# A gated convolution block's gradients: gradient of h interleaved with the weight gradients, and two queues held in program order

## The chip, the cores and the metric

The kernel runs on one core of a Trainium2 chip. The metric is the device time of one execution in microseconds. The core has five engines with a queue of instructions each: PE (TensorE, matmuls into PSUM), DVE (VectorE, elementwise), ACT (ScalarE, copies and functions), POOL (GpSimd, here mostly a queue that starts DMAs) and SP (SyncE, which only starts DMAs). PEld is PE's weight load, which runs beside the matmuls.

## The reference

All outputs of a forward pass and of its gradient (`jax.vjp`), S = 2048, D = 1024, F = 3584, bf16:

```python
x  = A_q
xn = layernorm(x)
# s: gated long convolution
kv = shift4(A_k, shift_k) * A_v
y  = irfft(rfft(kv, 2S) * rfft(ssm_k, 2S))[:S] + kv * ssm_D
s  = xn * y
# g: gated linear unit
h  = (xn @ w_gate) * (xn @ w_up)
g  = silu(h @ w_down)
out = x + s * g
# returned: out and the gradients of A_q, A_k, A_v, shift_k, ssm_k, ssm_D, w_gate, w_up, w_down
```

The Fourier transforms are done as matmuls with tables on PE (eight residues of the position), and short butterflies on VectorE.

## The kernel before

The program is one stream of traced instructions over all engines. A planner then puts each engine's instructions in an order, by priority and by its own estimates of when inputs are ready; on the chip each engine runs its queue in that order. `tc.high_priority` lifts instructions in it, `tc.issue_after(ins)` keeps a block's instructions behind `ins` on that engine.

The helpers `ld`, `st` and `sta` start a DMA from SP, GpSimd and ACT. `cld` is `st`. Nearly all VectorE work goes through `tt` (L199) and `stt` (L255), so these two lines carry many groups of the profile, which are told apart by their tiles.

Stages, in order:

1. Layer norm, and gate and up projections (L569, tile psg), with the forward convolution spread among them.
2. Multiplication by w_down and the gate's gradient (L961, function `gate`). It writes DY (gradient of the convolution's output) and DBM (gradient of h @ w_down) to DRAM.
3. The weight gradients of gate and up. F is cut into 14 slabs of 256. For each slab, `dh_half` computes the gradient of h for one half of the positions: two groups (g) of two PSUM tiles of 16 matmuls each (L1085), copied by ACT to dht (L1087), and VectorE multiplies the saved gate and up values by dht in place (tiles U<-U,dht); then the half is stored to DGd. `dw_slab` then makes the slab's weight gradients: 8 groups of 16 matmuls (L1100) that read these products, one ACT copy each (L1105), and stores of wb from ACT's queue.
4. The gradient of w_down: 14 slabs of 4 groups of 16 matmuls (L1201), copied by ACT to wbs (L1203, four buffers) and stored from SP's queue. The saved h of a slab is loaded two slabs ahead, from ACT's queue (`load_h`, U<-Hd). Beside it, SP issues the transposing DMAs that the last stage needs (L1160, L1167), from slab 1 on; each slab's are held behind the last store of wbs.
5. The gradient of xn (L1224) and the layer norm's gradient, with the gradient of k (`dk_units`) among it.

The backward convolution (`conv_backward`) is a generator that stages 3 and 4 draw forward. After each group of matmuls `btick` counts 1 (one PSUM tile of `dh_half`, 16 matmuls) or 2 (a dw or down group), and `make_pump` traces as much of the generator as keeps its share done. A generator's yields are its weights in estimated VectorE microseconds. First `dy_forward` transforms DY (8 units of `fwd8`) into DYFd. Then 16 units follow (8 of kind v, 8 of kind h). A unit's `main` loads A and B, multiplies them on VectorE (`product`, steps of 2.3, 2.5, 2.5, 2.5, 2.5) and does the inverse butterflies (`inv8`). A unit's `tail` does the last matmuls (psY: L404 for v, L901 for h), ACT copies and stores. `staggered` starts a unit's tail within the next unit's main, once more than 6.0 of its weights are done, and then alternates the two. At slab 11 of stage 4, `bdrain` traces what is left.

The order around the change was, in each slab `sl`: dh_half(2 sl + 1), dh_half(2 sl + 2) for the next slab, then dw_slab(sl). The multiply was lifted by `high_priority(60)`.

Of the kernel before, what the change touches and what calls it, by code (L numbers as in the profile page):

```python
# [19 lines left out]
def build_kernel(  # L20
# [11 lines left out]
    nc = tc.nc  # L32
# [27 lines left out]
    def ld(out, in_):  # L60
        return nc.sync.dma_start(out=out, in_=in_)

    def st(out, in_):
        return nc.gpsimd.dma_start(out=out, in_=in_)

# [127 lines left out]
    def pr(t, i, j):  # L193
        if j > i:
            return t[:, i:j + 1:j - i, :]
        return t[:, i:(j - 1 if j > 0 else None):j - i, :]

    def tt(o, a, b, op):
        V.tensor_tensor(o, a, b, op)  # L199

# [52 lines left out]
    def stt(o, a, f, b):  # L253

        V.scalar_tensor_tensor(o, a, f, b, op0=MUL, op1=ADD)  # L255

    def fwd8(x, X, wp, psp):

        W = wp.tile([P, 16, 256], F32, name="W16")
        C = wp.tile([P, 4, 256], F32, name="W4")  # L260
        for i in range(2):
            SP = wp.tile([P, 2, 2, 512], F32, name="SP", bufs=2)
            for j in range(2):
                r = 2 * i + j
                ps = psp.tile([P, 2, 2, 256], F32, name="psF")
                cmm(ps[:, 0], T4[0], x, (r,))
                cmm(ps[:, 1], T4[0], x, (r + 4,))
                nc.scalar.copy(out=SP[:, :, j], in_=ps[:].rearrange("p s k x -> p s (k x)"))
                yield 0.1
            s, q = [SP[:, j].rearrange("p a (k x) -> p (a k) x", k=2) for j in range(2)]  # L270
            tt(W[:, 4 * i:4 * i + 4, :], s, q, ADD)
            tt(W[:, 4 * i + 8:4 * i + 12, :], s, q, SUB)
            yield 2.5
        tt(C[:], W[:, 0:4, :], W[:, 4:8, :], ADD)
        tt(W[:, 0:4, :], W[:, 0:4, :], W[:, 4:8, :], SUB)
        yield 2.4
        dft4(C[:], W[:, 0:4, :], X, 0)
        yield 2.8

        d0, d2r = W[:, 8:10, :], W[:, 13:11:-1, :]  # L280
        tt(C[:, 0:2, :], d0, d2r, ADD)
        tt(d0, d0, d2r, SUB)
        re, im = W[:, 10:15:4, :], W[:, 11:16:4, :]
        tt(C[:, 2:4, :], re, im, ADD)
        tt(W[:, 12:14, :], im, re, SUB)
        yield 2.8
        q, pr_ = C[:, 2:4, :], W[:, 13:11:-1, :]
        tt(W[:, 10:12, :], q, pr_, ADD)
        tt(W[:, 14:16, :], q, pr_, SUB)
        stt(pr(X, 2, 15), W[:, 10:15:4, :], C8, C[:, 0:2, :])  # L290
        stt(pr(X, 10, 7), W[:, 10:15:4, :], -C8, C[:, 0:2, :])
        yield 2.9
        stt(pr(X, 6, 11), W[:, 11:16:4, :], C8, d0)
        stt(pr(X, 14, 3), W[:, 11:16:4, :], -C8, d0)
        yield 1.5
    FWD8_W = 0.4 + 2 * 2.5 + 2.4 + 2.8 + 2.8 + 2.9 + 1.5

# [502 lines left out]
    def dy_forward(cx, cs):  # L800
        def load(ds):
            x = cx.tile([P, NB, P], BF16, name="dyx")
            cld(x[:], DYd[ds])
            return x
        nx = load(0)
        for ds in range(8):
            x = nx
            if ds < 7:
                nx = load(ds + 1)
            X = cs.tile([P, 16, 256], BF16, name="DX")  # L810
            yield from fwd8(x, X, cs, ps_c3)
            st(DYFd[ds], X[:])

    def conv_backward():
# [54 lines left out]
        for n in range(16):  # L869
            yield from staggered(main(n), tl, 6.0)  # L870
            tl = tail(n)
# [6 lines left out]
    def dkv_tail(ds, G, tiles, ew):  # L878
        v, ksh = tiles
        y = ew.tile([P, NB, P], BF16, name="yl")  # L880
        for rp in range(4):
            ps = inv8_rows(G, ps_y4[0], rp)
            nc.scalar.copy(out=by_res(y[:], rp), in_=rowps(ps))
        yield 0.4
        tt(v[:], v[:], y[:], MUL)
        tt(ksh[:], ksh[:], y[:], MUL)
        for c in range(2):
            cs_ = slice(8 * c, 8 * c + 8)
            st(DKSHd[ds, 1024 * c:1024 * c + 1024, :].rearrange("(u r) d -> u r d", r=8), v[:, cs_, :])
            st(o_dv[:, c, :, ds * P:(ds + 1) * P], ksh[:, cs_, :])  # L890
        yield 2.5

    def dh_tail(ds, G, ew):
        ho = ew.tile([P, 2, P, 8], BF16, name="yl")
        for c in range(2):
            for rq in range(2):
                ps = ps_y4[0].tile([P, 4, P], F32, name="psY")
                for i in range(4):
                    r = 4 * rq + i
                    for k in range(2):  # L900
                        nc.tensor.matmul(ps[:, i, :], G[:, 2 * r + k, c * P:(c + 1) * P], TI[:, 0, r, k, :],  # L901
                                         start=(k == 0), stop=(k == 1))
                nc.scalar.activation(ho[:, c, :, 4 * rq:4 * rq + 4].rearrange("p u r -> p r u"), ps[:], ACT.Copy, scale=WSC)
        yield 0.4
        nc.scalar.copy(out=ddo[:, ds:ds + 1], in_=ho[:, 0, 0, 0:1])
        st(o_dssmk[ds * P:(ds + 1) * P, :], ho[:].rearrange("p c u r -> p (c u r)"))
        yield 0.1

# [42 lines left out]

    C_TOTAL = 8 * FWD8_W + 16 * (PROD_W + INV8_W) + 8 * 1.4 + 8 * 2.9 + 8 * 0.5
    bpump, bdrain = make_pump(conv_backward(), C_TOTAL)

# [114 lines left out]
    def btick(n):  # L1069
        bcnt[0] += n  # L1070
        bpump((bcnt[0] - 10) / (BT - 10))

    def dh_half(k, wdt):

        sl, hf = divmod(k, 2)
        dgu = DGU[k]
        for g in range(2):
            bs = slice(4 * g, 4 * g + 4)
            dht = bg.tile([P, 4, SLW], BF16, name="dht", bufs=3)
            for e in range(2):  # L1080
# [6 lines left out]
                nc.scalar.copy(out=dht[:, 2 * e:2 * e + 2].rearrange("p b f -> p (b f)"), in_=ps[:])  # L1087
                flush(2)
                btick(1)
            with tc.high_priority(60):  # L1090
                tt(dgu[:, :, bs], dgu[:, :, bs], dht[:].unsqueeze(1).to_broadcast([P, 2, 4, SLW]), MUL)

        ld(DGd[sl, :, 1024 * hf:1024 * hf + 1024, :].rearrange("a (u b) f -> u a b f", u=P), dgu)
        return dgu

    def dw_slab(sl, dgus):
        for dc in range(DC):
# [8 lines left out]
            if dc % 2 == 1:  # L1106
                fs, rows = slice(sl * SLW, (sl + 1) * SLW), slice((dc - 1) * P, (dc + 1) * P)
                for a, dst in enumerate((o_dwg, o_dwu)):
                    sta(dst[rows, fs].rearrange("(c p) f -> p c f", p=P), wb[:, :, a])
            flush(2)  # L1110
            btick(2)

    def load_h(sl):
        h = u8(HSL[sl % 3], "p (b f) -> p b f", b=NB)
        sta(h, Hd[sl])
        hs[sl] = h
# [8 lines left out]
    for k in (3, 4):  # L1125
        gu_in(k)
    first = dh_half(0, wdt)
    DBM = [u8(q, a=4) for q in (10, 8, 4, 5)]
    HSL = (3, 11, 6)
    hs = {}  # L1130
    for sl in range(NSL):
        dgus = [first, dh_half(2 * sl + 1, wdts[sl])]
        if sl + 2 < NSL:
            wdts.append(load_wdt(sl + 2))
        if sl + 1 < NSL:
            first = dh_half(2 * sl + 2, wdts[sl + 1])
        else:

            load_h(0)
            for q in range(4):  # L1140
                ld(DBM[q], DBMd[512 * q:512 * q + 512, :].rearrange("(b u) d -> u b d", u=P))
            load_h(1)
        dw_slab(sl, dgus)
        for k in (2 * sl + 5, 2 * sl + 6):
# [27 lines left out]
    for k in range(NSL):  # L1172
        if k + 2 < NSL:
            load_h(k + 2)
        with tc.issue_after(wst.ins) if k > 0 else nullcontext():
            if k in (1, 2, 3, 4, 5):
# [3 lines left out]
        if k == 11:  # L1180

            bdrain()
            tip.release()
            gw = pool("gw", 1)
# [11 lines left out]
        for f in range(2):  # L1196
# [8 lines left out]
            f0 = k * SLW + f * P  # L1205
            wst = ld(o_dwd[f0:f0 + P, :], wbs)
    for p_ in (ps_y4[0], ps_b, wo):
# [144 lines left out]
```

## Time and profile before

| what | value |
|---|---|
| median of 13 runs | 2067.99 us (2048.18 to 2097.93) |
| the profiled execution | 2056.26 us |
| its span, first to last instruction | 2054.5 us |
| PE busy | 1969.4 us (96%) |
| VectorE busy | 1411.8 us (69%) |
| ACT busy | 703.0 us (34%) |
| GpSimd busy | 305.4 us (15%) |
| mean granted PE clock | 0.986 |

Within the span, stage 3 begins at about 770 us, stage 4 at 1415, and stage 5 at about 1628. A group of the profile reads: line, engine, operation, tiles written and read, shapes, count; then busy time in us and the mean of one in ns; then the idle time of the engine just before them and what ended most of it. A wait reads: engine and line that waited, what it waited for, the sum in us, how often, and the longest. A timeline reads: start and length in us, engine, line, operation, tiles, shapes, count, and in brackets the idle time before it.

### The profile page before, as it was taken

The page shows a single profiled execution, that of the slowest core. Times are in us where ns is not written, and L with a number is a line of the kernel's source. Part 1 is how long each engine was busy: PE and PEld are TensorE (multiplying, and loading weights), DVE is VectorE, ACT ScalarE, POOL GpSimd, SP SyncE. Part 2 cuts the span into 40 slices and gives each one's busy share as a digit, 9 for nine tenths or more (in the row PEclk, how much of TensorE's full clock was granted, in tenths as well). Part 3 has the DMA queues.
Part 4 walks back from the last instruction along what each step waited for, and adds up shares of the span by engine and source line. Part 5 has one row for each costly group of instructions (what it writes and reads, how often), then busy time and mean ns, then how long its engine had stood idle before and what let it go on. Part 6 is the DMA issues. An engine that isn't in the chain of part 4 may idle for free.

```text
span 2054.5 us, 27733 instructions
## 1 busy us (share of the span) xinstructions
PE 1969.4 (96%) x11288; PEld 1054.2 (51%) x11288; DVE 1411.8 (69%) x1576; ACT 703.0 (34%) x962; POOL 305.4 (15%) x480
## 2 busy tenths in 40 slices
PE   6999999999999999999899899999899999989998
PEld 3455555545544446666555556654444444444443
DVE  7779898978836556887999889897574034434343
ACT  4655554546432234343222222334335101101112
POOL 3322222111112111001111221000000001010110
PEclk9999999999999999999999999999999999999999
DMA  9686666557699987665776676765999999392931
GB/s 300 228 279 222 203 217 214 199 186 243 222 299 291 292 286 272 202 217 195 265 247 209 209 253 214 245 240 154 154 246 204 202 209 230 96 191 88 218 84 57
DMA packets 422528, 440.74 MB, mean 215 GB/s; under 512 B 248960, under 2 KB 336824, under 8 KB 408576
## 3 DMA queue, kind: packets, MB, share of 16 engines
q1 hardware_dynamic: 331488, 203.72, 39.8%
q0 software_dynamic: 42112, 176.51, 25.7%
q10 hardware_dynamic: 48800, 58.73, 9.2%
q8 instruction: 88, 1.44, 0.3%
q14 instruction: 40, 0.33, 0.0%
HBM read 198.72 MB, written 189.83 MB: 189 GB/s over the span
## 4 chain that ended last, share of the span: by engine, by line
PE 43%; DVE 22%; issue 20%; DMA 7%; POOL 3%; SPq 3%; ACT 2%; ACTq 0%; POOLq 0%; DVEq 0%
PE psx L1224 17%; PE psb L1201 7%; PE psg L569 6%; DVE W L199 6%; PE psb L1100 6%; DVE m L199 4%; DVE HX L199 3%; PE psb L1085 2%; PE psF L221 2%; DVE KX L199 2%; DVE A L199 2%; DVE U L199 2%; SPq L1167 2%; DMA out_dram<-wbs 1%; SPq L1160 1%
## 5 line engine op out<-in xcount | busy, mean ns | idle before, releaser
L569 PE MATMUL psg<-wslab,U 128*128 128x512 bf16 x1792 | 414.7, 384 | 7.9 <-ACT U L542 3.8
L1100 PE MATMUL psb<-U,U 128*128 128x512 bf16 x1792 | 396.4, 381 | 13.2 <-DVE U L199 13.2
L1224 PE MATMUL psx<-U,dgut 128*128 128x512 bf16 x1536 | 338.1, 381 | 10.0 <-DVE dxn L199 5.5
L1100 PEld LDWEIGHTS <-U 128*128 128x128 bf16 x1792 | 176.0, 98 | 221.5 <-issue 19.1
L1224 PEld LDWEIGHTS <-dgut 128*128 128x128 bf16 x1792 | 174.4, 98 | 222.9 <-issue 17.0
L569 PEld LDWEIGHTS <-U 128*128 128x128 bf16 x1792 | 174.5, 99 | 199.9 <-issue 14.1
L1201 PE MATMUL psb<-U,U 128*128 128x512 bf16 x896 | 197.4, 383 | 7.0 <-ACT wbs L1203 7.0
L1085 PE MATMUL psb<-wdt,U 128*128 128x256 bf16 x1792 | 199.9, 273 | 1.1 <-ACT bm L979 1.1
L571 ACT CAST gut<-psg 128x512 bf16<-128x512 f32 x224 | 131.3, 587 | 201.8 <-PE psg L569 187.2
L1085 PEld LDWEIGHTS <-U 128*128 128x128 bf16 x1792 | 175.5, 98 | 24.6 <-issue 1.4
L961 PE MATMUL psbm<-U,ht 128*128 128x512 bf16 x784 | 169.9, 379 | 0.0
L1105 ACT CAST wb<-psb 128x512 bf16<-128x512 f32 x112 | 66.4, 596 | 300.2 <-PE psb L1100 291.5
L199 DVE TENSOR_TENSOR W<-SP 128x1024 f32<-128x1024 f32 x96 | 113.0, 1221 | 62.8 <-ACT SP L236 34.1
L1201 PEld LDWEIGHTS <-U 128*128 128x128 bf16 x896 | 88.2, 99 | 113.8 <-issue 7.0
L199 DVE TENSOR_TENSOR W<-W 128x1024 f32<-128x1024 f32 (+1 forms) x144 | 139.2, 985 | 2.8
L199 DVE TENSOR_TENSOR dka<-dkh,Wbc 128x1024 bf16<-128x1024 bf16 x16 | 11.1, 692 | 187.8 <-DMA dkh<-DKSHd 187.8
L1247 ACT ACTIVATE dx_t<-dxn 128x1024 bf16<-128x1024 f32 (+1 forms) x17 | 17.1, 1007 | 349.8 <-DVE dxn L199 296.2
L199 DVE TENSOR_TENSOR m<-A,B 128x2048 bf16<-128x2048 bf16 (+1 forms) x48 | 73.2, 1576 | 80.0 <-DMA B<-KFd 28.9
L961 PEld LDWEIGHTS <-ht 128*128 128x128 bf16 x784 | 76.6, 98 | 91.8
L1087 ACT CAST dht<-psb 128x512 bf16<-128x512 f32 x112 | 65.2, 586 | 128.6 <-PE psb L1085 111.7
L1203 ACT CAST wbs<-psb 128x512 bf16<-128x512 f32 x56 | 33.2, 621 | 137.7 <-DMA out_dram<-wbs 69.5
L199 DVE TENSOR_TENSOR U<-U,dht 128x2048 bf16<-128x2048 bf16 x56 | 68.3, 1219 | 15.1 <-ACT dht L1087 15.1
(202 smaller groups left out, 2300.2 us busy)
## 6 DMA issues: line engine op xcount, KB each, us to landing
U<-GUd SPq DMA_DIRECT2D x28, 1024.0 KB, 7.4
DGd<-U SPq DMA_DIRECT2D x28, 1024.0 KB, 5.2
GUd<-gut ACTq DMA_DIRECT2D x54, 512.0 KB, 4.3
A<-DYFd POOLq DMA_DIRECT2D x16, 1024.0 KB, 7.1
out_dram<-wb ACTq DMA_DIRECT2D x112, 128.0 KB, 3.1
U<-Hd ACTq DMA_DIRECT2D x14, 1024.0 KB, 8.5
Hd<-hN POOLq DMA_DIRECT2D x54, 256.0 KB, 4.1
HTd<-hT POOLq DMA_DIRECT2D x54, 256.0 KB, 4.0
```

The source lines that it names most:

```text
L199: V.tensor_tensor(o, a, b, op)
L221: nc.tensor.matmul(ps[:, k].rearrange("p (c d) -> p c d", c=2), T[:, r, k, :], xr[:, r], start=(n == 0), stop=(n == len(rs) - 1 and (first ...
L569: gu_mm[0] = nc.tensor.matmul(ps[:], XNT[q][:, dc, qi * P:(qi + 1) * P], w[:, dc].rearrange("p a f -> p (a f)"), start=(dc == 0), stop=(dc ...
L571: nc.scalar.copy(out=gut[:, :, i], in_=ps[:].rearrange("p (a f) -> p a f", a=2))
L961: nc.tensor.matmul(ps[:, dh * 512:(dh + 1) * 512], ht(fc)[:, i * P:(i + 1) * P], WD[fc // 4][:, fc % 4, dh * 512:(dh + 1) * 512], start=(f ...
L1085: nc.tensor.matmul(ps[:, x * SLW:(x + 1) * SLW], DBMT[2 * hf + g][:, dc, (b % 4) * P:(b % 4 + 1) * P], wdt[:, dc, :], start=(dc == 0), sto ...
L1087: nc.scalar.copy(out=dht[:, 2 * e:2 * e + 2].rearrange("p b f -> p (b f)"), in_=ps[:])
L1100: nc.tensor.matmul(ps[:], XN[b // 4][:, b % 4, dc * P:(dc + 1) * P], dgus[b // 8][:, :, b % 8], start=(b == 0), stop=(b == NB - 1))
L1105: nc.scalar.copy(out=wb[:, dc % 2].rearrange("p a f -> p (a f)"), in_=ps[:])
L1167: nc.sync.dma_start_transpose(out=t[:, 2 * i:2 * i + 2], in_=DGd[2 * j + i, a, 512 * g:512 * g + 512, :])
L1201: nc.tensor.matmul(ps[:], h[:, b, f * P:(f + 1) * P], DBM[b // 4][:, b % 4, dh * 512:(dh + 1) * 512], start=(b == 0), stop=(b == NB - 1))
L1224: nc.tensor.matmul(ps[:, dh * 512:(dh + 1) * 512], t[n][:, f, i * P:(i + 1) * P], WGU[n][:, f, dh * 512:(dh + 1) * 512], start=(n == 0 and ...
```

## The change

- `PIN` and `PINQ`: from the start of stage 3 to slab 11 of stage 4, every `tt` and `stt` on VectorE, and every DMA of `st` and `cld` on GpSimd's queue, is kept in the order in which it is traced.
- `dh_half` becomes a generator. The first slab's two halves run ahead. After that, one group (g) of the next slab's halves follows each of the first four matmul groups of `dw_slab`. The multiply is put on a list (`todo`), is traced behind the next group's ACT copy, and loses its high priority.
- `fwd8`: its matmuls and the ACT copies to SP move to `fwd8_half` and are traced within the unit before; DY is loaded two units ahead.
- `staggered` gets 7.0 instead of 6.0; the tails' yields become 0.0, and the v tail has one more step ahead of its multiplies.
- `dh_tail`: ACT copies PSUM in plain order; GpSimd then copies it into the transposed order (tile ho), and copies the one column of ddo.
- Stage 4: h is loaded from SP's queue and wbs is stored from ACT's. The transposing loads of a slab are held behind the load of h.

The diff, cut to its core:

```diff
 def st(out, in_):
-    return nc.gpsimd.dma_start(out=out, in_=in_)
+    ins = nc.gpsimd.dma_start(out=out, in_=in_)
+    if PINQ[0]:
+        tc.keep_in_program_order(ins)
+    return ins
...
 def tt(o, a, b, op):
-    V.tensor_tensor(o, a, b, op)
+    ins = V.tensor_tensor(o, a, b, op)
+    if PIN[0]:
+        tc.keep_in_program_order(ins)
...
+def fwd8_half(x, i, wp, psp):
+    SP = wp.tile([P, 2, 2, 512], F32, name="SP", bufs=2)
+    for j in range(2):
...
+        nc.scalar.copy(out=SP[:, :, j], in_=ps[:].rearrange("p s k x -> p s (k x)"))
+    return SP
...
         tt(W[:, 0:4, :], W[:, 0:4, :], W[:, 4:8, :], SUB)
+        ahead(0)
         yield 2.4
         dft4(C[:], W[:, 0:4, :], X, 0)
+        ahead(1)
         yield 2.8
...
-            yield from staggered(main(n), tl, 6.0)
+            yield from staggered(main(n), tl, 7.0)
...
 def dkv_tail(ds, G, tiles, ew):
...
-    yield 0.4
+    yield 0.0
+    yield 0.0
     tt(v[:], v[:], y[:], MUL)
...
 def dh_tail(ds, G, ew):
-    ho = ew.tile([P, 2, P, 8], BF16, name="yl")
+    hr = ew.tile([P, 2, 8, P], BF16, name="yl")
+    ho = ew.tile([P, 2, P, 8], BF16, name="ho")
...
-            nc.scalar.activation(ho[:, c, :, 4 * rq:4 * rq + 4].rearrange("p u r -> p r u"), ps[:], ACT.Copy, scale=WSC)
-    yield 0.4
-    nc.scalar.copy(out=ddo[:, ds:ds + 1], in_=ho[:, 0, 0, 0:1])
+            nc.scalar.activation(hr[:, c, 4 * rq:4 * rq + 4], ps[:], ACT.Copy, scale=WSC)
+    yield 0.0
+    nc.gpsimd.tensor_copy(ho[:], hr[:].rearrange("p c r u -> p c u r"))
+    nc.gpsimd.tensor_copy(ddo[:, ds:ds + 1], hr[:, 0, 0, 0:1])
     st(o_dssmk[ds * P:(ds + 1) * P, :], ho[:].rearrange("p c u r -> p (c u r)"))
...
+def after_group(n):
+    flush(2)
+    while todo:
+        todo.pop(0)()
+    btick(n)
...
-            with tc.high_priority(60):
-                tt(dgu[:, :, bs], dgu[:, :, bs], dht[:].unsqueeze(1).to_broadcast([P, 2, 4, SLW]), MUL)
-        ld(DGd[sl, :, 1024 * hf:1024 * hf + 1024, :].rearrange("a (u b) f -> u a b f", u=P), dgu)
+            def multiply(g=g, dht=dht):
+                bs = slice(4 * g, 4 * g + 4)
+                tt(dgu[:, :, bs], dgu[:, :, bs], dht[:].unsqueeze(1).to_broadcast([P, 2, 4, SLW]), MUL)
+                if g == 1:
+                    ld(DGd[sl, :, 1024 * hf:1024 * hf + 1024, :].rearrange("a (u b) f -> u a b f", u=P), dgu)
+            todo.append(multiply)
+            yield
...
-def dw_slab(sl, dgus):
+def dw_slab(sl, dgus, others):
     for dc in range(DC):
...
-            btick(2)
+            after_group(2)
+            next(others, None)
...
 def load_h(sl):
-    sta(h, Hd[sl])
+    h_ld[0] = ld(h, Hd[sl])
...
+PIN[0] = PINQ[0] = True
+for k in range(2):
+    run(dh_half(k, wdt))
+todo.pop()()
 for sl in range(NSL):
-    dgus = [first, dh_half(2 * sl + 1, wdts[sl])]
...
+    def halves():
+        for k in (2 * sl + 2, 2 * sl + 3):
+            if k < 2 * NSL:
+                yield from dh_half(k, wdts[sl + 1])
+    dw_slab(sl, [DGU[2 * sl], DGU[2 * sl + 1]], halves())
...
-        with tc.issue_after(wst.ins) if k > 0 else nullcontext():
+        with tc.issue_after(h_ld[0].ins):
...
-            wst = ld(o_dwd[f0:f0 + P, :], wbs)
+            sta(o_dwd[f0:f0 + P, :], wbs)
```

## The prediction

> **What bounds the kernel now.** I read the page, then PE's own waits, then busy time by stretch, then the instruction order around the longest stall.
>
> Part 1 of the page, and two of its groups:
>
> ```profile
> span 2054.5 us, 27733 instructions
> PE 1969.4 (96%) x11288; PEld 1054.2 (51%) x11288; DVE 1411.8 (69%) x1576; ACT 703.0 (34%) x962; POOL 305.4 (15%) x480
> ...
> L1100 PE MATMUL psb<-U,U 128*128 128x512 bf16 x1792 | 396.4, 381 | 13.2 <-DVE U L199 13.2
> ...
> L1203 ACT CAST wbs<-psb 128x512 bf16<-128x512 f32 x56 | 33.2, 621 | 137.7 <-DMA out_dram<-wbs 69.5
> ```
>
> PE is the bound: no other engine passes 69%. The change removes no matmul, so it can only win back PE's idle time and the slow clock that follows it. The whole idle sum is 2054.5 − 1969.4 = 85.1 us, of which only some lies in the changed stages. PE's waits, all causes:
>
> ```profile
> PE psb L1100 <- DVE U L199: 13.2, 7, 4.1
> PE psb L1201 <- ACT wbs L1203: 7.0, 2, 6.0
> PE psY L404 <- DVE B L255: 6.0, 2, 5.8
> ```
>
> Busy time in four stretches (backward convolution's first part; its products beside the weight gradients; the down-weight stage; the last stage), then three of the 50 us stretches with a low clock. Columns: PE, PEld, DVE, ACT, POOL busy, granted clock, DMA share, GB/s.
>
> ```profile
> 770.00:980.00 210.00, 208.88 (x1384) 135.03 (x1384) 156.61 (x191) 77.62 (x112) 16.77 (x29) 1.00 0.67 225
> 980.00:1415.00 435.00, 415.87 (x2563) 248.78 (x2562) 396.48 (x365) 128.55 (x193) 61.74 (x93) 0.98 0.70 229
> 1415.00:1628.00 213.00, 206.01 (x1067) 97.67 (x1065) 112.02 (x110) 76.36 (x80) 8.21 (x14) 0.98 1.03 194
> ...
> 1000.00:1050.00 50.00, 44.02 (x273) 27.31 (x272) 49.52 (x46) 12.15 (x22) 8.07 (x12) 0.93 0.67 221
> 1150.00:1200.00 50.00, 43.20 (x238) 24.23 (x237) 42.85 (x39) 10.45 (x18) 7.50 (x11) 0.90 0.69 212
> 1450.00:1500.00 50.00, 44.04 (x216) 20.38 (x215) 30.27 (x28) 15.24 (x16) 1.59 (x3) 0.93 1.16 187
> ```
>
> Between 980 and 1415 PE idles 435 − 415.87 = 19.1 us. The clock costs more on top: 50 x (1 − 0.93) = 3.5 us, 50 x (1 − 0.90) = 5.0, and 50 x (1 − 0.97) = 1.5 in 1350:1400, together 10.0. The down stage idles 7.0, its clock costs 3.5, and 2.2 us at L1224 wait for the last wbs copies. So the ceiling is 19.1 + 10.0 + 7.0 + 3.5 + 2.2 = 41.8 us.
>
> The longest stall, as the timelines of VectorE, PE and GpSimd tell it:
>
> ```profile
> 1149.39 4.56 DVE L199 TENSOR_TENSOR m<-A,B 128x4096 bf16<-128x4096 bf16 x3 [8.55 <-DMA B<-HFd]
> ...
> 1160.17 1.22 DVE L199 TENSOR_TENSOR U<-U,dht 128x2048 bf16<-128x2048 bf16 x1
> ...
> 1161.44 1.86 PE L1100 MATMUL psb<-U,U 128*128 128x512 bf16 x4 [4.08 <-DVE U L199]
> 1166.04 1.86 PE L1100 MATMUL psb<-U,U 128*128 128x512 bf16 x4 [2.73 <-DVE U L199]
> ...
> 1137.60 0.97 POOL L64 DMA_DIRECT2D out_dram<-kshl  x1
> 1138.38 0.74 POOL L64 DMA_DIRECT2D B<-HFd  x1
> ```
>
> B's load leaves GpSimd's queue at 1138.38, as the unit before ends on VectorE, because it stands behind that unit's tail stores. VectorE stops 8.55 us; the four multiplies U<-U,dht stand behind the product, and PE waits for them.
>
> **The change, part by part.**
>
> *Program order on VectorE and GpSimd.* Held order puts B's load after the tail's stores right behind the product (12.3 of a unit's 28.9 in the pump's weights), so 16.6 remain before it is needed; its median landing is 8.7 us (HFd) or 10.0 (KFd). What is queued behind: the load stands behind DKSHd and dv stores that wait for two VectorE multiplies issued at the same place (2 x 1.22 us). VectorE's group m<-A,B of 4096 lost 80.0 us, nearly all to B; between 979 and 1407 some 34 of 428 us. Starts of products run 979.3 to 1407.3 for 12 units: 35.7 us each, 32.8 without those stops. PE gives a unit about 20 ticks of 1.73 us (16 matmuls at 216 ns for two ticks) plus 1.8 us of psY: 36.5 us. VectorE then has 3.7 us to spare per unit instead of 0.8.
>
> *Interleaving.* Before, the last multiply for a slab has one dh_half (64 matmuls at 109 ns, 7.0 us) and 8 x 0.216 = 1.7 us ahead of its reader. After, dh groups follow the first four dw groups, and each multiply is issued behind the next group. The last is issued behind dw group 4, so groups 5, 6, 7 give 3 x 3.45 = 10.4 us plus 1.7. The earlier three have more. PE's work is the same 1792 + 1792 matmuls. At the start weight gradients begin after two halves, not three: 770 + 14 = 784. Their XN loads leave SP by 769.2, median landing 9.3 us, so about 5 us cover them; with that cover gone the stall would be one landing's rest, once.
>
> *What stays in this stretch.* Going from dy to the products, VectorE waits for stores and loads whatever the order (7.56 us before L199's first m<-A,B, and gaps of 2.3 to 2.6 us ahead of three multiplies). Held order places the multiplies behind that product. I keep one stall like the one at 1001 (5.0 us) and a clock dip of 3.4. So 29.1 − 8.4 = 20.7 us won.
>
> *fwd8 a unit ahead.* VectorE's 28.6 us of waits for SP go. PE does not wait there (208.88 of 210 busy), so 0; it cushions the passage above. The lag 6.0 to 7.0 changes nothing: product steps stand at 4.8 and 7.3, so both start the tail at 7.3. The added empty step moves VectorE's tail multiplies one step later.
>
> *dh tail.* ACT's strided copies:
>
> ```profile
> L903 ACT ACTIVATE yl<-psY 128x512 bf16<-128x512 f32 x32 | 74.8, 2717 | 0.0
> ...
> L163 POOL TENSOR_TENSOR m<-f,tcol 128x1024 int32<-128x1024 int32 x1 | 1.9, 1909 | 0.0
> ```
>
> ACT gets 32 x (2.717 − 0.604 of L883's plain copy) = 67.6 us free, worth 0 directly: ACT waits for PE. GpSimd gets eight strided copies of 2048 elements, not in this trace. From below, a plain write, IOTA 1.0 us per 1024: 2.0 us. From above, L163 doubled, 3.8, times ACT's strided ratio 4.5: 17 us. I take 3, near the contiguous rows, since here only the read is strided. The row alone says 8 x 3 = 24 us hidden on an engine 15% busy. A rule speaks against it: by the Trainium skill's page "SBUF — State Buffer", section "Who interferes with whom", a VectorE instruction with two SBUF inputs and a GpSimd instruction that reads SBUF exclude one another for the whole instruction. No row here shows that. By the rule each copy adds 3 us to a VectorE unit, inside the 3.7 to spare: still 0. At 17 us it would not fit (rival below).
>
> *Down stage: stores wbs to ACT's queue, loads h to SP's.* ACT issues 28 x 0.4 us and waits for nothing new there. But h now queues behind the transposes:
>
> ```profile
> 1430.05 36.94 SPq L1160 DMA_TRANSPOSE U<-in_B_w_gate_dram  x1
> 1467.08 1.47 SPq L61 DMA_DIRECT2D out_dram<-wbs  x2
> 1468.65 14.03 SPq L1160 DMA_TRANSPOSE U<-in_B_w_up_dram  x1
> 1482.77 1.00 SPq L61 DMA_DIRECT2D out_dram<-wbs  x2
> 1483.86 16.01 SPq L1160 DMA_TRANSPOSE U<-in_B_w_gate_dram  x1
> ```
>
> With the stage's start as 0 and 13.8 us a slab, SP is free at 13.8 + 36.9 = 50.7, 64.8 and 80.8. Loads h(4), h(5), h(6) leave then, land 8.5 later (59, 73, 89), and are wanted at 55, 73 (after the slip) and 87: 6 us late in all, and a dip of 3.4. Won: 12.7 − 9.4 = 3.3 us. Bounds: +12.7 if h is never late, −20 or worse below.
>
> *Sum.* 20.7 + 3.3 = 24 us. The profiled execution took 2056.26 (span 2054.5 and 1.8 around it): 2032. It lies 11.7 under the median of 2067.99, so against the median 2044.
>
> **A clock rule.** Row: 5.79 us idle at 1001 brought 3.5 us of clock, 6.8 within 1150:1200 brought 5.0, while 2.09 at 1303 brought none and 2.03 + 1.25 near 1385 brought 1.5. The skill's page "TensorE: Matmul & The Clock Gate" (section "What's actually happening") asks for one idle window of about 3.4 us before the clock halves. By it the pair near 1385 would cost nothing; by the row, 1.5. I price by the row: a stall of over 3 us costs half as much again or more.
>
> **Rivals.**
>
> *B, all of it goes* (chance 0.12): for it, B's load has 6 us of reserve and h(4) to h(6) miss by few us. 2068 − 42 = 2026.
>
> *C, stalls move* (0.15): VectorE in program order waits at the passage, then recovers 3.7 us a unit, 5 units for 18 us; each slab in that time finds its multiplies late. Against: 12.1 us of lead. Four slabs at 5 us use up the gain: 2065.
>
> *D, slower: h behind the transposes on SP* (0.13). With m the mean SP time of a transposing slab (k = 1 to 9), the load issued at k = 9 lands at 13.8 + 8m + 8.5 and is wanted at 151.8: late by 8m − 129.5. Before, the five of L1160 average 17.3 and the four dgut slabs less, so it is only early slabs that miss. The gain is gone at m = 18.8; at m = 20 it is 30.5 late against 20.7 won, and with dips some 15 slower: 2083.
>
> *E, slower: the strided copy at 13 us, excluding VectorE* (0.12). In four units of the slab stretch 13 − 3.7 = 9.3 us each reach PE: 37; in four of the down stage, without multiplies, some 5 each: 20. Less 24: 2068 + 33 = 2101; at 10 us a copy 4 x 6.3 + 4 x 3 − 24 = 13, so 2081. It decides from about 8.5 us a copy.
>
> **How the numbers follow.** A (above) 0.48, its own range 2032 to 2056. A and B are faster, 0.60; C is the same, 0.15; D and E slower, 0.25. The bound of 0.5% is 10.3 us, about what a measurement here can tell from no change. The range leaves out the far half of B and the far half of D and E: 2022 to 2086. The time is A's, 2044.
>
> **What would show it.** Right: L1100's wait for DVE U under 4 us, m<-A,B of 4096 waiting under 25 us, clock dips before 1415 from three to one, L903 near 600 ns, the weight stage ending near 1394. Wrong: PE L1201 waiting for DMA U<-Hd by more than 15 us (D); GpSimd copies over 8 us, with longer VectorE instructions beside them (E); DVE U waits above 10 us in the first slabs after the passage (C).

## The result, and the profile after

The changed kernel takes 2039.52 us (median of 11 runs, 2030.3 to 2056.9) against 2067.93 for the kernel before. The ratio is 0.9886, 95% interval 0.986 to 0.9911: 1.1% faster, some 24 us by the ratio and 28 by the medians, because the ratio leaves out executions in a slower state. The forecast was 2044 in a range of 2022 to 2086.

The page of the changed kernel, the parts and groups that answer to those shown of before:

```profile
span 2039.1 us, 27740 instructions
PE 1972.6 (97%) x11288; PEld 1056.1 (52%) x11288; DVE 1438.1 (71%) x1576; ACT 647.8 (32%) x954; POOL 344.7 (17%) x496
...
L1136 PE MATMUL psb<-U,U 128*128 128x512 bf16 x1792 | 397.8, 380 | 0.0
```

L1136 is the weight-gradient matmul, L1100 before. Its 13.2 us of waits for VectorE's multiplies are gone. VectorE is busy 26 us longer with the same 1576 instructions; that is taken up below. PE's longest waits in the changed stages name other things than before:

```profile
PE psb L1244 <- DMA U<-Hd: 5.0, 1, 5.0
PE psb L1244 <- ACT wbs L1246: 4.5, 2, 2.9
...
PE psF L230 <- DMA dyx<-DYd: 3.6, 1, 3.6
PE psY L420 <- DVE B L264: 3.0, 2, 2.0
```

L1244 is the down stage. Busy time by stretch, first before (slab stage, down stage), then after (775 to 985 and 985 to 1403 are the slab stage, then the down stage and the last). Columns as in the prediction.

```profile
770.00:1415.00 645.00, 624.75 (x3945) 383.81 (x3945) 553.09 (x555) 206.17 (x305) 78.51 (x122) 0.98 0.69 228
1415.00:1630.40 215.40, 206.17 (x1068) 97.78 (x1067) 112.02 (x110) 77.43 (x82) 8.21 (x14) 0.98 1.03 195
```

```profile
775.00:985.00 210.00, 206.41 (x1345) 132.42 (x1344) 156.07 (x190) 76.66 (x110) 16.72 (x29) 0.98 0.66 222
985.00:1403.00 418.00, 414.92 (x2602) 250.98 (x2601) 393.80 (x352) 108.91 (x192) 76.17 (x98) 1.00 0.76 238
1403.00:1625.00 222.00, 208.39 (x1068) 98.11 (x1067) 141.46 (x124) 42.85 (x77) 33.47 (x25) 0.98 0.98 201
1625.00:2039.00 414.00, 404.12 (x2038) 186.04 (x2037) 159.44 (x214) 57.51 (x85) 38.54 (x61) 0.99 0.66 148
```

The slab stage went from 645 us to 628, PE idle in it from 20.3 us to 6.7. The down stage went from 215.4 to 222, so in these two executions it got longer. The last stage went from 424.1 to 414. The stage ahead of all edits took 770.0 and 774.9. So these two profiles differ by 15.4 us, not by the 28 of the medians: the profiled execution of before lies 11.7 us under its own median. Where the rest sits is a question for the runs.

### The profile page after: what moved, and what is told of

The parts are those of the page before. It is cut to its first block, busy times and chain, and to the rows that moved or that the text cites. A ratio compares the mean times of both kernels' runs of the same rounds, so it can differ in the third digit from the quotient of the medians.

```text
span 2039.1 us, 27740 instructions
## 1 busy us (share of the span) xinstructions
PE 1972.6 (97%) x11288; PEld 1056.1 (52%) x11288; DVE 1438.1 (71%) x1576; ACT 647.8 (32%) x954; POOL 344.7 (17%) x496
## 4 chain that ended last, share of the span: by engine, by line
PE 64%; issue 12%; DVE 12%; DMA 4%; SPq 2%; POOL 2%; ACT 1%; ACTq 0%; POOLq 0%; DVEq 0%
PE psx L1267 18%; PE psb L1136 18%; PE psb L1119 8%; PE psg L585 7%; PE psb L1244 6%; DVE W L206 3%; DVE HX L206 3%; PE psF L230 2%; DVE m L206 2%; DVE KX L206 2%; SPq L1209 1%; DMA U<-Hd 1%; SPq L1202 1%; DVE U L206 1%; PE psdk L964 1%
## 5 line engine op out<-in xcount | busy, mean ns | idle before, releaser
L585 PE MATMUL psg<-wslab,U 128*128 128x512 bf16 x1792 | 420.7, 388 | 6.9 <-ACT U L558 3.9
L1136 PE MATMUL psb<-U,U 128*128 128x512 bf16 x1792 | 397.8, 380 | 0.0
L1267 PEld LDWEIGHTS <-dgut 128*128 128x128 bf16 x1792 | 174.0, 98 | 212.7 <-issue 5.4
L1136 PEld LDWEIGHTS <-U 128*128 128x128 bf16 x1792 | 175.7, 98 | 199.6 <-issue 1.6
L1244 PE MATMUL psb<-U,U 128*128 128x512 bf16 x896 | 199.7, 385 | 12.4 <-DMA U<-Hd 5.0
L1119 PE MATMUL psb<-wdt,U 128*128 128x256 bf16 x1792 | 207.1, 274 | 1.1 <-DMA U<-XNd 1.1
L206 DVE TENSOR_TENSOR W<-W 128x1024 f32<-128x1024 f32 (+1 forms) x144 | 149.6, 1057 | 3.0
L1244 PEld LDWEIGHTS <-U 128*128 128x128 bf16 x896 | 88.6, 99 | 121.1 <-issue 14.3
L206 DVE TENSOR_TENSOR dka<-dkh,Wbc 128x1024 bf16<-128x1024 bf16 x16 | 11.1, 692 | 170.4 <-DMA dkh<-DKSHd 170.4
L206 DVE TENSOR_TENSOR m<-A,B 128x2048 bf16<-128x2048 bf16 (+1 forms) x48 | 73.4, 1576 | 30.8 <-DMA B<-KFd 16.4
```

Of the source, the lines that this page charges most:

```text
L206: ins = V.tensor_tensor(o, a, b, op)
L585: gu_mm[0] = nc.tensor.matmul(ps[:], XNT[q][:, dc, qi * P:(qi + 1) * P], w[:, dc].rearrange("p a f -> p (a f)"), start=(dc == 0), stop=(dc ...
L1119: nc.tensor.matmul(ps[:, x * SLW:(x + 1) * SLW], DBMT[2 * hf + g][:, dc, (b % 4) * P:(b % 4 + 1) * P], wdt[:, dc, :], start=(dc == 0), sto ...
L1136: nc.tensor.matmul(ps[:], XN[b // 4][:, b % 4, dc * P:(dc + 1) * P], dgus[b // 8][:, :, b % 8], start=(b == 0), stop=(b == NB - 1))
L1244: nc.tensor.matmul(ps[:], h[:, b, f * P:(f + 1) * P], DBM[b // 4][:, b % 4, dh * 512:(dh + 1) * 512], start=(b == 0), stop=(b == NB - 1))
L1267: nc.tensor.matmul(ps[:, dh * 512:(dh + 1) * 512], t[n][:, f, i * P:(i + 1) * P], WGU[n][:, f, dh * 512:(dh + 1) * 512], start=(n == 0 and ...
```

## The experiments

The theory after the first profiles was the prediction's: held order brings B's loads forward and the interleaving gives the multiplies a longer lead, and together they empty the slab stage; the exchange of queues in the down stage is worth little. Its rivals: the interleaving alone does it; ACT's relief does it; the exchange costs time.

The stage times of each run's profiled execution, from the first matmul of one stage to the first of the next (us), with the ratio of times to the kernel before on the same chip:

| kernel | median, profiled execution | ahead | slab stage | PE idle in it | down stage | PE idle in it | last | ratio (95%) |
|---|---|---|---|---|---|---|---|---|
| before | 2067.93, 2056.26 | 770.0 | 645.0 | 20.3 | 215.4 | 9.2 | 424.1 | 1 |
| changed | 2039.52, 2040.89 | 774.9 | 628.0 | 6.7 | 222.1 | 13.6 | 414.1 | 0.9886 (0.986 to 0.9911) |
| after_again | 2038.81, 2053.30 | 776.8 | 625.6 | 5.8 | 234.7 | 27.5 | 414.4 | 0.9901 (0.9869 to 0.9933) |
| queues_back | 2057.98, 2054.85 | 775.2 | 625.7 | 6.3 | 232.8 | 28.0 | 419.3 | 0.9989 (0.9943 to 1.0035) |
| no_pins | 2038.85, 2042.96 | 771.4 | 627.1 | 7.5 | 222.8 | 13.5 | 419.9 | 0.9891 (0.9853 to 0.9929) |
| act_tail | 2035.29, 2046.33 | 776.2 | 628.3 | 7.2 | 223.4 | 17.9 | 416.6 | 0.9897 (0.9842 to 0.9951) |
| before_queues | 2061.08, 2055.01 | 773.6 | 646.0 | 21.6 | 219.7 | 15.5 | 413.9 | 0.9883 (0.9821 to 0.9946) |
| before_pins | 2032.78, 2026.23 | 768.8 | 629.5 | 8.8 | 209.6 | 7.5 | 416.6 | 0.9743 (0.9681 to 0.9806) |
| pins_again | 2036.93, 2036.77 | 775.6 | 631.4 | 10.4 | 211.4 | 9.4 | 416.7 | 0.9806 (0.9762 to 0.985) |
| inter_only | 2057.61, 2032.64 | 770.3 | 631.4 | 10.9 | 212.7 | 10.5 | 416.4 | 0.9823 (0.9732 to 0.9914) |
| inter_queues | 2053.38, 2056.15 | 774.9 | 631.4 | 10.5 | 233.7 | 27.7 | 414.5 | 0.9839 (0.9754 to 0.9924) |
| plain_wgu | 2034.54, 2032.80 | 773.4 | 625.8 | 6.1 | 216.5 | 11.4 | 415.3 | 0.9813 (0.9761 to 0.9865) |
| late_wgu | 2051.37, 2051.39 | 775.5 | 625.7 | 6.1 | 234.6 | 27.7 | 413.9 | 0.9889 (0.9854 to 0.9924) |
| pins_late | 2043.65, 2043.16 | 776.7 | 626.6 | 7.8 | 219.7 | 15.8 | 418.4 | 0.9859 (0.9821 to 0.9897) |

The runs come from several chips, and the kernel before differed between them: 2067 us beside after_again, queues_back, no_pins and act_tail, 2085 beside before_queues, before_pins, inter_only and inter_queues, 2079 beside the rest. The changed kernel ran only where the kernel before took 2067 or 2068. A ratio carries from chip to chip only if a chip slows all kernels alike, and that is not shown: the stage ahead, which no edit touches, took 768.8 to 774.9 us where the kernel before took 2085, and 771.4 to 776.8 where it took 2067. Some profiled executions also lie far from their kernel's median, that of inter_only by 25 us.

**The changed kernel again.** No edit.

> The changed kernel itself, as the mark for the runs beside it: 0.986 of the kernel before, near 2040 us. All theories expect the same; what its profile tells is whether the stage times of the first one (slab stage 628 us, down stage 222, last stage 414) come again. If the last stage's 10 us are chance, it returns to about 424 here.

Measured: 2038.81 us. Its profiled execution has a span of 2051.5 us, 12.4 more than the first, and the table says where: slab stage 625.6 and last stage 414.4 as before, but 234.7 in the down stage instead of 222.1. PE's waits there:

```profile
PE psb L1244 <- DMA U<-Hd: 14.9, 1, 14.9
...
PE psb L1244 <- ACT wbs L1246: 7.2, 2, 5.8
```

So one load of h came 14.9 us late instead of 5.0, of the same program. It had stood in SP's queue behind a long transpose:

```profile
1460.28 35.46 SPq L1202 DMA_TRANSPOSE U<-in_B_w_gate_dram  x1
1495.84 0.53 SPq L61 DMA_DIRECT2D U<-Hd  x1
```

The slab stage repeats within 3 us from execution to execution; the down stage does not. The last stage stayed short.

**Queues back.**

```diff
-        h_ld[0] = ld(h, Hd[sl])
+        sta(h, Hd[sl])
...
-        with tc.issue_after(h_ld[0].ins):
+        with tc.issue_after(wst.ins) if k > 0 else nullcontext():
...
-            sta(o_dwd[f0:f0 + P, :], wbs)
+            wst = ld(o_dwd[f0:f0 + P, :], wbs)
```

> The changed kernel with h loaded from ACT's queue and wbs stored from SP's again. My prediction gave this part 3.3 us of gain, so +3 us over the changed kernel (about 2043). The rival, from the profile after (down stage 222 us against 215): the exchange costs time, since h is late by 5.0 us with a dip of the clock; then this one is 5 to 10 us faster than the changed kernel (2030 to 2035).

Measured: 2057.98 us, 19 us over the changed kernel, and no longer distinguishable from the kernel before. Both expectations missed, the rival's by its sign. The slab stage kept its gain (625.7), so the loss lies behind it. PE waits there for ACT, whose copies wait (30.5 us at the longest) for the landing of stores that stand behind the transposes on SP; SP's queue comes last:

```profile
PE psb L1244 <- ACT wbs L1246: 17.9, 1, 17.9
...
PE psx L1267 <- ACT wbs L1246: 8.8, 1, 8.8
```

```profile
1454.66 39.19 SPq L1202 DMA_TRANSPOSE U<-in_B_w_gate_dram  x1
1493.94 3.81 SPq L61 DMA_DIRECT2D out_dram<-wbs  x2
```

The profiles alone do not measure the 19 us: the down stage of 232.8 us is 10.7 over the first profile of the changed kernel and 1.9 under the second, which was the longest of its nine executions. The 19 us rest on the medians.

**Nothing held.**

```diff
-    PIN[0] = PINQ[0] = True
+    PIN[0] = PINQ[0] = False
```

> The changed kernel with nothing held in program order. Theory 1 (the held order brings B's loads forward and so frees the multiplies): the waits for B come back, 50 to 80 us of VectorE, and with the multiplies no longer lifted PE waits 15 us or more for them: +15 to +30 us, 2055 to 2070. Theory 2 (the interleaving's longer lead alone did it): VectorE waits for B but PE does not, within 5 us of the changed kernel.

Measured: 2038.85 us, the changed kernel's time; slab stage 627.1. Theory 2, that the interleaving's longer lead alone suffices, met its number. VectorE does stop for loads, though less than theory 1 said: 22.2 us between 980 and 1398. The stop named issue ended as a load of B landed, 16.3 us after it was issued. PE waited for a multiply only once, at 1103.6, some 30 us after that stop. VectorE's waits, then PE's:

```profile
DVE m L206 <- issue: 12.6, 1, 12.6
DVE m L206 <- DMA B<-KFd: 9.6, 3, 5.0
```

```profile
PE psb L1136 <- DVE U L206: 4.7, 1, 4.7
```

**The old tail of h.**

```diff
-                nc.scalar.activation(hr[:, c, 4 * rq:4 * rq + 4], ps[:], ACT.Copy, scale=WSC)
+                nc.scalar.activation(ho[:, c, :, 4 * rq:4 * rq + 4].rearrange("p u r -> p r u"), ps[:], ACT.Copy, scale=WSC)
...
-        nc.gpsimd.tensor_copy(ho[:], hr[:].rearrange("p c r u -> p c u r"))
-        nc.gpsimd.tensor_copy(ddo[:, ds:ds + 1], hr[:, 0, 0, 0:1])
+        nc.scalar.copy(out=ddo[:, ds:ds + 1], in_=ho[:, 0, 0, 0:1])
```

> The changed kernel with the old tail of h: ACT's strided copies, no copy on GpSimd. VectorE loses the 26 us in which the profile after shows instructions of 3.97 to 4.74 us beside GpSimd's copies. Theory 1: these lay in VectorE's spare time, and ACT's 68 us too, so the time is within 5 us of the changed kernel. Rival A: the exclusion of VectorE reached PE, this one is 8 us or more faster. Rival B: ACT's relief was part of the gain, this one is 8 us or more slower, with PE waits for ACT copies.

Measured: 2035.29 us, ratio 0.9897 beside the changed kernel's 0.9901 on the same chip; slab stage 628.3. Theory 1's number is met; neither rival's 8 us is there. The run takes out ACT's relief and GpSimd's copies together, so it shows that the two come to nothing in sum, not that each does. What the copies do to VectorE is told in the last section.

**The exchange of queues alone**, on the kernel before.

> The kernel before with the exchange of queues alone (h from SP's, wbs from ACT's). New theory: two gains that add, about 19 us from the exchange in the down stage and about 18 us from the interleaving in the slab stage; then 19 us under the kernel before (about 2049), slab stage unchanged at about 645. Rival: the exchange pays only with the rest; then within 6 us of the kernel before. My prediction's own figure for it was 3.3 us.

Measured: 2061.08 us where the kernel before took 2085.47 on that chip, ratio 0.9883: 24 us faster, with the slab stage as before (646.0, and PE psb L1100 <- DVE U still at 12.4 us). The theory of two gains that add met its sign and about its size. The interval is wide, 11 to 37 us, and the profile does not show where the gain lies: its down stage of 219.7 us is longer than the 215.4 of the one profile of before.

**Held order alone**, on the kernel before.

```diff
+        ins = nc.gpsimd.dma_start(out=out, in_=in_)
+        if PINQ[0]:
+            tc.keep_in_program_order(ins)
...
+    PIN[0] = PINQ[0] = True
     first = dh_half(0, wdt)
```

> The kernel before with VectorE's and GpSimd's order held as traced, its order of halves and slabs unchanged. My prediction's mechanism (held order brings B's loads forward, VectorE stops less, PE waits less): slab stage 630 or less, 10 us or more faster. Rival, from the run with nothing held: the order on those queues doesn't matter, the lead of the multiplies does; then slab stage 640 to 655 and the time within 10 us of the kernel before, or slower since the multiply is no longer lifted.

Measured: 2032.78 us, ratio 0.9743. The slab stage falls to 629.5. So the prediction's mechanism holds by itself too. A load of B was issued 20.0 us before the product that reads it (median of the second to the twelfth product), against 11.0 before; it was 17.3 in the changed kernel, 9.9 with nothing held. One such load on GpSimd's queue, and its product on VectorE, which did not wait:

```profile
1131.89 0.74 POOL L66 DMA_DIRECT2D B<-HFd  x1
```

```profile
1152.32 4.55 DVE L206 TENSOR_TENSOR m<-A,B 128x4096 bf16<-128x4096 bf16 x3
```

VectorE's waits between 980 and 1398, of this kernel; before, B<-HFd and B<-KFd cost 38.5 us in six stops, one of them (7.6 us) at the passage from dy to the products. Now one stop is left:

```profile
DVE U L206 <- ACT dht L1098: 18.3, 9, 4.3
DVE m L206 <- DMA B<-HFd: 17.9, 1, 17.9
```

That one is the passage, and there the multiply stands behind the product just as forecast. VectorE's order, and PE behind it:

```profile
980.88 2.29 DVE L206 TENSOR_TENSOR m<-A,B 128x4096 bf16<-128x4096 bf16 x1 [17.85 <-DMA B<-HFd]
983.09 1.22 DVE L206 TENSOR_TENSOR U<-U,dht 128x2048 bf16<-128x2048 bf16 x1
```

```profile
984.37 5.80 PE L1111 MATMUL psb<-U,U 128*128 128x512 bf16 x15 [6.05 <-DVE U L206]
```

**The interleaving alone**, on the kernel before (`dh_half` as a generator, `todo`, `dw_slab` with `others`, the loop over slabs; the multiply loses its high priority with it).

> The kernel before with the interleaving of halves and slabs alone: nothing held in order, no matmuls of fwd8 ahead, the old tails, the old queues. New theory: the slab stage falls to about 627 (the lead does it alone), the down stage stays long: 8 to 19 us faster, 2049 to 2060. Rival: the other parts (fwd8 ahead, tails, order) are needed; slab stage 638 or more.

Measured: 2057.61 us, ratio 0.9823; slab stage 631.4. No wait for the multiplies is left; one of 7.7 us for DVE B is. So the interleaving suffices in the slab stage without the matmuls of fwd8 ahead, the tails or held order. It also left VectorE fewer stops, though the loads of B were issued no earlier (10.1 us ahead of their product): behind the passage two of at most 4.7 us, where before had six of up to 8.7.

```profile
DVE m L199 <- DMA B<-HFd: 17.1, 1, 17.1
...
DVE m L199 <- DMA B<-KFd: 7.6, 2, 4.7
```

So this run does not separate the longer lead from the fewer stops. The run with nothing held speaks for the lead too: behind the passage VectorE's products stopped 22.2 us there and PE waited 4.7 us for multiplies, against 34.1 and 13.2 before. But that is no separate test. The down stage, expected to stay long, took 212.7 us in the profiled execution, which is the shortest of the four by 22 us.

**Interleaving and exchange together.**

> Interleaving and exchange of queues together, nothing else of the change. New theory: all of the gain, within 6 us of the changed kernel (2034 to 2046). Rival: held order, fwd8 ahead or the tails carry a part; then 2050 or more.

Measured: 2053.38 us, ratio 0.9839. The theory's number (2034 to 2046) missed, and the rival's (2050 or more) was met on a chip where the kernel before took 2085. By the ratio it is level with the interleaving alone, within intervals of nearly 1% either way: no gain from the exchange is seen here, and PE lost 12.6 us to a late h in the down stage of 233.7. So the two gains do not simply add: the slab stage's is there in each kernel that has either edit, the exchange's depends on the kernel.

**What makes the down stage so uneven?** In the changed kernel's first profile, SP's queue and then GpSimd's:

```profile
1432.51 0.32 SPq L61 DMA_DIRECT2D U<-Hd  x1
1432.89 23.38 SPq L1202 DMA_TRANSPOSE U<-in_B_w_up_dram  x1
1456.36 0.53 SPq L61 DMA_DIRECT2D U<-Hd  x1
1456.95 11.87 SPq L1202 DMA_TRANSPOSE U<-in_B_w_gate_dram  x1
1468.91 1.64 SPq L61 DMA_DIRECT2D U<-Hd  x1
1470.59 30.60 SPq L1202 DMA_TRANSPOSE U<-in_B_w_up_dram  x1
```

```profile
1437.64 0.53 POOL L66 DMA_DIRECT2D A<-DYFd  x1 [6.01 <-DVE W L206]
...
1470.47 0.53 POOL L66 DMA_DIRECT2D A<-DYFd  x1 [6.01 <-DVE W L206]
```

The transposes that took 23.4 and 30.6 us are those beside which A was loaded; these two loads of A took 20.8 and 26.1 us to land, where the median of all 16 is 9.0. The load of h behind the first of them left at 1456.36, 10 us after its turn (the end of slab 2). The one behind the next transpose left at 1468.91, 7 us after its turn, and took 25.5 us to land; for it PE waited. Two kernels ask whether the pair is the cause.

**Plain loads for the transposes.**

```diff
-        nc.sync.dma_start_transpose(out=store, in_=(B_w_gate, B_w_up)[a][:, j * 512:(j + 1) * 512])
+        ld(store, B_w_down[j * 512:(j + 1) * 512, :].rearrange("(c p) d -> p c d", p=P))
```

> The changed kernel with the 14 transposing loads of w_gate and w_up replaced by plain loads of the same bytes (from w_down), so the gradient of A_q is made from other weights. Theory: in the down stage a transposing load and a 1 MB load of A or B from GpSimd's queue, when both are under way, each take 20 to 39 us, and this makes h or the stores of wbs late; without the transposes there: no load of A, B or h over 15 us, down stage 200 to 208 us instead of 222 to 235, and 15 to 25 us faster than the changed kernel. Rival: bytes alone make the jam; then loads of 20 us and more stay and the down stage stays above 215.

Measured: 2034.54 us, ratio 0.9813, by the ratio 15 to 18 us under the changed kernel; the times themselves, from different chips, differ by 4 to 5 us. In the first 150 us of the down stage no load of A or B takes over 10.3 us and none of h over 8.2, and PE does not wait there at all. So in this execution the same bytes did not jam, and with the transposes they did. The down stage of 216.5 us misses the 200 to 208: its waits (5.2, 1.5 and 1.0 us for wbs) now lie behind slab 11, where transposes of dgut and GpSimd's loads for the gradient of k run together and land after 24 to 26 us.

**The transposes later.**

```diff
-            if k in (1, 2, 3, 4, 5):
-                load_wgu(k - 1, u8((7, 0, 1, 9, 2)[k - 1], a=4))
+            for n in {8: (0,), 9: (1, 2), 10: (3, 4)}.get(k, ()):
+                load_wgu(n, u8((7, 0, 1, 9, 2)[n], a=4))
```

> The changed kernel with the first five transposing loads of w_gate and w_up moved from slabs 1 to 5 of the down stage to slabs 8 to 10, behind the last loads of A and B. Theory (overlap with A and B makes the jam): transposes at 4 to 9 us each, down stage 203 to 212, 10 to 20 us faster than the changed kernel (ratio to before 0.978 to 0.984). Rival: the transposes jam with h and the stores too, or come too late for the last stage: PE waits there 10 us or more at L1267 for U<-in_B_w, no gain (0.986 to 0.992).

Measured: 2051.37 us, ratio 0.9889: no gain, so the number of the theory missed. Its mechanism held in part: away from the transposes the two loads of A take 6.1 and 8.2 us, and h 5.3 to 8.4. But two of the five moved transposes held SP for 14.3 and 24.1 us instead of 4 to 9, and behind slab 11 five transposes now stand more closely with the late ones and with the loads for the gradient of k, and PE has one long wait there, as long as what was to be won:

```profile
PE psb L1244 <- ACT wbs L1246: 19.6, 1, 19.6
```

**Held order alone, again, and with the later transposes.**

> The kernel before with only VectorE's and GpSimd's order held, once more, on more executions. If the 0.974 of the first time is this kernel's own: 0.971 to 0.979, and the whole change (0.989 and 0.990) is worth less than its part. If it was one chip's state or few executions: 0.982 to 0.990, like the change.

> The kernel before with VectorE's and GpSimd's order held and the five transposing loads moved to slabs 8 to 10. Theory: slab stage 629, down stage 203 to 212; as fast as or faster than held order alone: 0.968 to 0.977. Rival (the move helps nothing or brings waits in the last stage): at or above held order alone, 0.977 or more.

Measured: 2036.93 us, ratio 0.9806, for held order alone, between the two expectations; 2043.65, ratio 0.9859, with the later transposes, which again cost more than they win, as the rival said. In both of its runs held order alone was faster than the kernel before. By the ratio, 0.9743 and 0.9806, it is also faster than the whole change at 0.9886 and 0.9901; by the times, 2032.78 and 2036.93 against 2039.52 and 2038.81, it leads by 2 to 7 us. The two never ran on the same chip, so whether the part beats the whole stays open. What the same chip shows is that held order alone (2026.2 to 2039.1) was faster than the interleaving and the exchange together (2041.2 to 2066.2). Its down stage took 209.6 and 211.4 us, with the old queues: there the loads of B and A leave some 2 us ahead of the transpose of slab 2, which then takes 12.9 us, and A lands after 13.5.

## Why the prediction was right, step by step

**Slab stage, 20.7 us forecast.** Right in mechanism and near in size: 17 us in the profiles (645.0 to 628.0), the waits for multiplies gone, the clock's loss halved. What the prediction did not see is that its two causes are redundant. It charged the gain to held order and interleaving together; the runs show 629.5 and 631.4 with held order alone, 631.4 with the interleaving alone, 627.1 with all but the held order, and 628.0 and 625.6 with all. With held order the loads of B leave earlier and VectorE's stops behind the passage are gone, as forecast; VectorE's order and GpSimd's queue were held together, so which of the two counts more is not shown. The interleaving does it by the longer lead and by fewer stops of VectorE; how much each counts is not shown, nor why the stops are fewer. One reading was wrong without harm: of the 80.0 us that VectorE's products lost, the page puts 51.7 down to B and 28.2 to "issue"; the 34 us of the slab stage, on which the sum rests, stand.

**The signs.** PE's waits for the multiplies went to none, and the plain copies of the h tail took 601 ns. Others missed by little: the products of 4096 still waited 30.8 us instead of under 25, two dips of the clock were left before the down stage instead of one, it began at 1402.9 us instead of 1394 (4.9 of these lay ahead of all edits), and of VectorE's 28.6 us of waits for SP 11.1 remained.

**One stall kept at the passage, 5.0 us and a dip.** VectorE stopped 13.9 us there in the changed kernel; PE then lost 3.0 us at psY, less than kept. With held order alone it lost 6.05 at the multiply. Another stall appeared, 3.6 us for the first load of DY, with a dip; it is 2.7 to 4.5 us in nearly all runs, the one with the exchange alone too, so it is no effect of the interleaving.

**The dh tail, 0 us.** Right in sum (act_tail); each alone was not tested. My 3 us for a copy was too low: it took 4.13 on average. Rival E decided from 8.5 us, so it did not come.

**Down stage, 3.3 us.** This is the step that was mis-sized. The price named was a late h, 6 us and a dip; PE waited 5.0 us with a dip in the first execution, and that nearness is luck. The sum let h(6) leave SP 80.8 us into the stage and land 8.5 us later. In the first execution it left at 66.0 and took 25.5 to land. In the second it left at 93.4 and took 8.1; PE waited 14.9 us, just under the 15 that the prediction gave as the sign of its rival D. So the time in SP's queue was wrong in the second, and in the first the landing of 8.5 us, a median over all slabs: in the trace of before, two loads of h beside the longest transpose had taken 33.1 and 22.3 us, and the late ones of no_pins and inter_queues took 34.3 and 29.6. The gain on the other side was larger too. The prediction read one execution of before, in which the stage took 215.4 us, as the stage's time. By the medians the exchange is worth 19 us in the changed kernel and 24 in the kernel before, and nothing is seen beside the interleaving alone.

**The sum.** 24 us were forecast, 28 came by the medians and 15.4 between the two profiles, so the nearness is partly luck. In the profiles the slab stage won 17.0 us, the down stage lost 6.7 where 3.3 were to be won, the last stage won 10.0 that no step had, and the stage ahead lost 4.9. How the 28 of the medians divide among the stages is not shown.

**The last stage** lost its 5.5 us wait at L1224 for DVE dxn and a dip. It takes 413.9 to 419.9 us in every kernel run here, also those with one edit. The one profile of before with 424.1 cannot tell whether that stall belongs to the kernel before or to that execution; this stays open.

**Against the median.** The step from 2032 for the profiled execution to 2044 for the median moved the sum by the 11.7 us by which the profile of before was lucky. That was sound: the measured median is 2039.5, and the span of the changed kernel's two profiles, 2039.1 and 2051.5, is not 2032 either.

## What to carry to other kernels

When PE waits for an instruction that stands behind a stopped one, there are two cures to try, to unblock the queue or to lengthen the lead. Here either edit was enough, so try each alone before taking both. Stages whose time repeats (the slab stage, within 3 us) can be summed from one profile; a stage that swings by 12 us or more between executions of the same program has to be read from several. An exchange of queues moves the wait to whatever stands behind the slow DMA then, so ask which of the two can bear it, and time many executions: here one profile with the exchange and one without put the down stage at 234.7 and 232.8 us, while the medians put the kernels 19 us apart. A load's median landing is no price for a load that lands beside a slow one. And let the kernels that are to be compared run on the same chip.

## What the runs showed of the hardware that was not expected

**A transpose beside a load from GpSimd's queue.** In the changed kernel a 1 MB transposing load held SP for 4.4 to 8.5 us where no 1 MB load from GpSimd ran beside it. Beside one it took up to 30.6 us there and up to 39.2 in queues_back, and the loads beside these 26 to 36. With plain loads of the same bytes, or with the transposes moved away, the loads of A and h in the same place took 5 to 10 us. What makes it mild or bad was not settled: a load 2 us ahead of the transpose went with 12.9 us, one 4 to 5 us behind with 16 to 27, one 2 us behind with 14.1 (act_tail), and one 0.5 us behind with 36.9 (the kernel before).

**GpSimd's copy shuts VectorE out.** The same 3 us of the changed kernel, GpSimd's queue and then VectorE's:

```profile
1426.58 3.69 POOL L931 COPY ho<-yl 128x2048 bf16<-128x2048 bf16 x1
```

```profile
1424.30 2.29 DVE L206 TENSOR_TENSOR W<-A 128x2048 f32<-128x2048 bf16 x1
1426.62 5.99 DVE L206 TENSOR_TENSOR W<-W 128x1024 f32<-128x1024 f32 x2
```

An instruction W<-W takes 1.22 us elsewhere; here one of the two took 4.73, its own time and 3.5 us more, nearly the 3.65 us that the copy still ran. In each of seven of the eight copies one VectorE instruction with two SBUF inputs was longer by about the copy's remaining length, 23.5 us together; beside the eighth VectorE was idle. That is the exclusion that the Trainium skill's page "SBUF — State Buffer" (section "Who interferes with whom") states, and that the prediction could not show from the trace of before.

**The length of a stall alone did not decide whether the clock fell.** In the changed kernel PE idled 2.88 us from 1592.8, and the clock was at half from 1596.1 for 3.4 us; it idled 2.91 us from 1604.4, and the clock stayed. Columns as in the prediction, the granted clock third from the end:

```profile
1592.00:1600.00 8.00, 5.12 (x17) 1.93 (x16) 4.75 (x7) 1.07 (x2) 0.87 (x1) 0.79 1.24 308
1600.00:1612.00 12.00, 9.09 (x43) 4.02 (x42) 0.00 (x0) 1.07 (x2) 0.00 (x0) 1.00 1.10 231
```

In pins_late a stall of 2.29 us brought half clock for 3.4 us, and in before_queues one of 3.26 us brought none. By the page "TensorE: Matmul & The Clock Gate" (section "What's actually happening") one idle window of about 3.4 us is needed; here shorter stalls were enough, though not each time.
